# Two branches of softmax attention: projection moves on GpSimd's queue, and denominators moved and inverted ahead of the sums

## The chip, the core and the metric

One NeuronCore of a Trainium2 chip runs the whole program. The time is the device time of one execution, in microseconds (us). For the kernel before, three runs took 2023.84, 2019.86 and 2020.14 us; their median is 2020.14 us.

## The reference, cut to what matters

The same input x (2048 tokens, width 512) goes through two attention layers of 32 heads of width 16, and a gate mixes their outputs token by token. Branch a has one key and value head for all its query heads; branch b has its own for each.

```python
# B, S, D, H = 1, 2048, 512, 32; Dh = 16
g = sigmoid((x * gate_w).sum(-1, keepdims=True))
# a: k = x @ wk, v = x @ wv are shared by all 32 heads;  b: q, k, v per head from x @ wqkv
scores = einsum("bhqd,bhkd->bhqk", q, k) * Dh ** -0.5
p = softmax(scores, axis=-1)
o = einsum("bhqk,bhkd->bhqd", p, v)          # heads side by side, 512 wide
a_or_b = o.transpose(0, 2, 1, 3).reshape(B, S, D) @ wo
out = g * a + (1 - g) * b
```

The exponentials are the bulk: 2 branches x 32 heads x 2048 x 2048 of them.

## The kernel before, in words

**The stream of exps.** The work is cut into eight groups of eight heads, a0, b0, a1, b1 and so on to a3, b3. A group has two halves of 1024 queries. Within a half, four "banks" follow each other; a bank is four (head, block of 512 queries) pairs over all 16 tiles of 128 keys. ScalarE (ACT) takes two pairs' scores for one key tile at a time: one instruction on 128 x 1024 scores, called an exp below (line 533). There are 2048 of them, 256 to a group, 128 to a half, 32 to a bank. TensorE (PE) makes the scores of an exp (line 529) into one of two PSUM buffers, and multiplies the probabilities with the values (line 548, "P V") a few exps later. Ones stand beside the values, so the P V bank collects for each head 16 rows of sums and 16 rows of denominators. There is no pass for a maximum.

**The other work of PE** is put between the exps, one or two products of 216 planned ns at a time: projections of x to Q, K and V of the next head groups, twelve products each per block of 512 tokens (line 351; the helper's line 189 appears in the profile), and output projections, three products each (line 442, again line 189). They accumulate in that pair of the two P V bank pairs which is not in use ("spare"), so VectorE (DVE) has to empty a bank before PE can begin the next of them.

**After a projection** DVE adds the two half sums into a tile y (lines 193 and 194), clips it, and splits it into a high and a low fp16 part, hi and lo (lines 201 and 202). Then rows of hi and lo have to go to other partitions: for each Q or K tile of a head pair p, eight DMAs of 32 KB (line 338, function `lay`, "moves" below). A projection of 1024 tokens gives four `lay` calls. They go into a list, from which one is taken each three exps (line 124). All these DMAs are issued by SyncE's queue (SP), except the first ones of the program.

**After a P V bank** DVE copies it to a tile `raw` (lines 193, 194; `emptied`, line 553), and eight DMAs on SP move its 16-row pieces into oT (sums) and dT (denominators), alternating. When two banks are in, for each of four 128-token columns DVE runs `over`, the reciprocal of dT (line 462), and then `parts`: the product with oT, and the split into fp16 halves (lines 469 to 471). Then PE can make the output projection of these tokens (`o_unit`), and DVE adds it to the result (line 450).

**What sets the order.** All queues are in order. A planner (`_Tasks`) writes the program exp by exp: `now` counts exps, a clock adds planned ns for each piece, EXP is the planned length of an exp (904), `units` holds products with the earliest exp and a due exp, `side` holds DVE and GpSimd pieces with their earliest exp, and `moves` the `lay` calls. None of it waits for time on the chip; it sets the order alone.

**GpSimd (POOL)** splits each newly loaded weight into fp16 halves (`split_weight`, lines 205 to 207), about 12 exps into a half. Two or three buffers serve each kind of weight, so such a split can wait for PE to be done with an older weight.

Of the kernel before, what the change touches and what calls it, by code (L numbers as in the profile page):

```python
# [22 lines left out]
DH = 16  # L23
# [3 lines left out]
BLK = 512  # L27
ACT = 2
ROWS, COLS = 64, 32
EXP = 904  # L30
SCORES, HALF, PRODUCT = 213, 428, 216
FULL = 1500
LATE = 250
# [31 lines left out]
class _Tasks:  # L65
# [53 lines left out]
    def beside(self, until):  # L119
        while self.side and self.side[0][0] <= self.now and self.busy <= until:  # L120
            _, f, ns = self.side.popleft()
            f()
            self.given(ns)
        if self.moves and self.moved <= self.now - 3:
            self.moved = self.now
            self.moves.popleft()()

    def flush(self):
# [3 lines left out]
        while self.open or self.units or self.side:  # L132
# [5 lines left out]
            self.now += 100  # L138
            self.clock += 100 * EXP
            while self.product(1 << 20) and self.open:  # L140
# [12 lines left out]
def _fast(ctx, tc, x, wq_a, wk_a, wv_a, wo_a, wqkv_b, wo_b, gate_w, out, flag):  # L153
    nc = tc.nc
# [60 lines left out]
    todo = _Tasks()  # L215
# [158 lines left out]
    def q_units(src, gi, half, queues, late=None):  # L374
        def put(p):
            Q[src, gi, half, p] = ops.tile([P, 2 * BLK], F16, tag="Q", name=f"Q{src}{gi}{half}{p}", bufs=8)
            return Q[src, gi, half, p]

        return project(weights[src, gi, "q"], ("q", src, gi), f"{src}{gi}", f"q_{src}", 4 * gi + 2 * half, half,
                       ("hi", "lo", "hi", "lo"), put, queues, late)  # L380

    def k_units(gi, half, queues):
        def put(p):
            if half == 0:
                K[gi, p] = ops.tile([P, S], F16, tag="K", name=f"K{gi}{p}", bufs=4)
            return K[gi, p][:, half * 2 * BLK : (half + 1) * 2 * BLK]

        return project(weights["b", gi, "k"], ("k", "b", gi), f"k{gi}", "k_b", 4 * gi + 2 * half, half,
                       ("hi", "hi", "lo", "lo"), put, queues)

    def v_units(gi):

        w = weights["b", gi, "v"]

        def product(b, n):
            assert ("v", "b", gi) in ready
            c, (x_part, w_part) = n // 3, PARTS[n % 3]
            by_tiles(spare(), w[:, w_part, c * P : (c + 1) * P], xT[:, x_part, c, b * BLK : (b + 1) * BLK],
                     n == 0, n == 3 * NK - 1)
            if n < 3 * NK - 1:  # L400
                return
            y = ops.tile([P, BLK], F32, tag="y", name=f"yv{gi}{b}")
            v16 = ops.tile([P, 2, BLK], F16, tag="v16", name=f"v16{gi}{b}")
            added(y, spare(), UP ** -2)
            split(v16[:, 0], v16[:, 1], y)
            absmax("v_b", 4 * gi + b, y)
            todo.add([[lambda t=t: turned(b, v16, t) for t in range(4)]], todo.now + 4, todo.now, -400)

        def turned(b, v16, t):
            banks = spare()  # L410
            at = slice(t * DH * 4, (t + 1) * DH * 4)
            for part in range(2):
                for n in range(0, P, COLS):
                    for i, bank in enumerate(banks):
                        r = slice(ROWS * i, ROWS * (i + 1))
                        nc.tensor.matmul(bank[n : n + COLS, at], v16[r, part, t * P + n : t * P + n + COLS],
                                         ident16[r, r], start=t == part == 0, stop=t == 3 and part == 1)
            if t < 3:
                return
            for i, bank in enumerate(banks):  # L420
                o = bank[:, : 4 * ROWS].rearrange("p (t a b d) -> p t a b d", t=4, a=2, b=2)
                for hh in range(2):
                    nc.vector.tensor_scalar(vB[:, 4 * b : 4 * b + 4, 2 * i : 2 * i + 2, 2 * hh, :], o[:, :, :, hh, :],
                                            1 / UP, None, op0=ALU.mult)
            turns[gi] = turns.get(gi, 0) + 1
            if turns[gi] == 4:
                ready.add(("v", gi))

        return [[lambda b=b, n=n: product(b, n) for n in range(3 * NK)] for b in range(4)]

    turns = {}
    oT, dT, o16s = {}, {}, {}
# [23 lines left out]
    def norm_pieces(src, gi, half, t8, last):  # L456
        j, cols = t8 // 4, slice(t8 % 4 * P, (t8 % 4 + 1) * P)
        ends = last and half and j

        def over():  # L460
            d = dT[src, gi, half, j][:, cols]
            nc.vector.reciprocal(d, d)  # L462

        def parts():
            o, d = oT[src, gi, half, j][:, cols], dT[src, gi, half, j][:, cols]
            if t8 == 0:
                o16s[src, gi, half] = ops.tile([P, 2, 2 * BLK], F16, tag="o16", name=f"o16{src}{gi}{half}", bufs=3)
            o16 = o16s[src, gi, half][:, :, t8 * P : (t8 + 1) * P]
            nc.vector.scalar_tensor_tensor(o, o, UP, d, op0=ALU.mult, op1=ALU.mult)
            (nc.scalar.copy if ends else nc.vector.tensor_copy)(o16[:, 0], o)  # L470
            (nc.gpsimd if ends else nc.vector).tensor_sub(o16[:, 1], o, o16[:, 0])
            todo.add([o_unit(src, gi, 8 * half + t8, o16, last)], todo.now + 4,
                     todo.now + (64 if last and half else 300))

        return [over, parts]
# [30 lines left out]
    def gates():  # L506
# [9 lines left out]
    blocks = [(n, half, s, c, p, j, hh) for n in range(len(groups)) for half in range(2)  # L516
              for s, bank in enumerate(banks) for c in range(NT) for p, j, hh in bank]
# [35 lines left out]
    def emptied(m):  # L553
        quad = blocks[4 * m : 4 * m + 4]
        n, half, s, c = quad[0][:4]
        src, gi = groups[n]
        raw = ops.tile([P, BLK], F32, tag="raw", name=f"raw{src}{gi}{half}{s}", bufs=1)
        added(raw, aux[turn[0]], 1.0)
        j = quad[0][5]
        if s % 2 == 0:  # L560
            oT[src, gi, half, j] = ops.tile([P, BLK], F32, tag="oT", name=f"oT{src}{gi}{half}{j}")
            dT[src, gi, half, j] = ops.tile([P, BLK], F32, tag="dT", name=f"dT{src}{gi}{half}{j}")
        for i, (_, _, _, _, p, _, hh) in enumerate(quad):
            rows = slice((2 * p + hh) * DH, (2 * p + hh + 1) * DH)
            parts = (oT, dT) if src == "a" or hh == 0 else (dT, oT)
            for part, at in zip(parts, (32 * i, 32 * i + DH)):
                ends = 4 * m + 4 == len(blocks)
                queues = (nc.sync, nc.scalar, nc.sync, nc.scalar, nc.gpsimd) if ends else (nc.sync,)
                queues[at // DH % len(queues)].dma_start(part[src, gi, half, j][rows], raw[at : at + DH, :])  # L569
        last = n == len(groups) - 1  # L570
        if s % 2:
            todo.add_side([f for t8 in range(4 * j, 4 * j + 4) for f in norm_pieces(src, gi, half, t8, last)],
                          todo.now + (5 if last and half else 10), [950, 800])

    def flag_stats():
        absmax("v_a", 0, vA[:, :, :DH], AX.XY)
# [28 lines left out]
    def begin(n, half):  # L605

        src, gi = groups[n]
        now = todo.now
        start = lambda n, half: (512 * n + 256 * half) // ACT
        sync = (nc.sync,)  # L610
        if half == 0:
            todo.add(q_units(src, gi, 1, sync), now if n else 24, start(n, 1) - 24, 2200)
        if n == 0 and half == 0:
            todo.add_side(load_w(*groups[1]), now + 12, [0])
        if n + 2 < len(groups) and half:
            todo.add_side(load_w(*groups[n + 2]), now + 12, [0])
        if n + 1 == len(groups):
            if half:
                todo.add_side([flag_stats], now + 60, [9000])
                todo.add_side([flag_reduce], now + 75, [400])  # L620
                todo.add_side([flag_check], now + 90, [1500])
            return
        nxt = groups[n + 1]
        due = start(n + 1, 0) - 36
        if half == 0:
            if nxt[0] == "b":
                todo.add(k_units(nxt[1], 0, sync) + k_units(nxt[1], 1, sync), now + (12 if n else 40), due - 90, 2200)
                todo.add(v_units(nxt[1]), now + (12 if n else 40), due - 30, 1700)
        else:
            todo.add(q_units(*nxt, 0, sync), now + 6, due, 2200)  # L630

# [25 lines left out]
    while done < halves:  # L659
        u += 1  # L660
        todo.now, todo.clock = u, u * EXP
        if u < exps:
# [4 lines left out]
        for f in early.get(u, ()):  # L667
            f()
        end = (u + 1) * EXP
        if half_values(u) and done < u - 2 and u % 2:  # L670
# [147 lines left out]
```

## Time and profile before

| | before |
|---|---|
| median of three runs | 2020.14 us |
| the profiled execution's own time | 2015.9 us |
| its span, first to last instruction | 2014.1 us |
| busy: PE, ACT, DVE, POOL | 1872.3, 1897.1, 768.9, 92.6 us |
| mean granted TensorE clock | 0.98 |
| DMA issued by SP, mean busy share of the 16 engines | 11.6% |

The views used are: the page (busy time; groups of instructions with their count, mean and the idle time before them), the list of waits (who waited for whom: us in total, times, longest), and timelines of one engine (start, length, instruction; in brackets the idle time of the engine just before it and what ended it). "SPq" is the time in which SP's queue issues a DMA. In a timeline "x3" means that like instructions were merged in one row.

### The profile page before, as it was taken

The numbers are of one execution on the slowest core, as the hardware profiler recorded it, in microseconds if no ns is written. First come the engines' busy times: TensorE is split into PE (matmuls) and PEld (weight loads), VectorE is DVE, ScalarE is ACT, GpSimd is POOL, SyncE is SP. The second block draws the span as 40 slices with busy tenths as digits, with TensorE's granted clock in tenths as the row PEclk, the third lists the DMA queues.
The fourth block names the chain that finished last, engine by engine and source line by source line (L and its number), as shares of the span: only waits on it lengthen the run. The fifth ranks groups of instructions, "written<-read, shape, count | busy, mean of one in ns | idle before, by whom it ended". The sixth has DMA issues, their size and how long they took to land.

```text
span 2014.1 us, 127353 instructions
## 1 busy us (share of the span) xinstructions
PE 1872.3 (93%) x59664; PEld 1062.3 (53%) x59664; DVE 768.9 (38%) x1429; ACT 1897.1 (94%) x2071; POOL 92.6 (5%) x103
## 2 busy tenths in 40 slices
PE   7988998999998999999998999999999899999995
PEld 4544654554554655555454665555545465555442
DVE  4332443424143444434333344452423333444432
ACT  4987998999998999999998999999999899999994
POOL 5001000020000000020000000002000000000000
PEclk9999999999998999999999999999999899999997
DMA  4012011111011101111002201011101110111111
GB/s 139 12 39 54 15 25 29 27 29 35 14 33 41 36 21 26 35 31 28 21 16 47 47 11 36 18 28 35 35 12 29 40 29 16 34 29 36 35 32 32
DMA packets 55735, 65.00 MB, mean 32 GB/s; under 512 B 21440, under 2 KB 29632, under 8 KB 55200
## 3 DMA queue, kind: packets, MB, share of 16 engines
q1 hardware_dynamic: 53984, 55.66, 11.6%
q8 instruction: 469, 7.68, 1.6%
q0 software_dynamic: 528, 0.69, 0.2%
q14 instruction: 66, 0.54, 0.1%
q10 hardware_dynamic: 688, 0.43, 0.1%
HBM read 10.55 MB, written 4.19 MB: 7 GB/s over the span
## 4 chain that ended last, share of the span: by engine, by line
ACT 69%; PE 11%; issue 7%; SPq 7%; DVE 3%; DMA 2%; ACTq 0%; DVEq 0%; POOL 0%
ACT pr L533 69%; SPq L338 5%; PE aux L548 5%; PE sc L529 3%; PE aux L189 3%; SPq L569 2%; DMA dTa<-rawa 1%; DMA acc<-in_A_x_dram 0%; DVE acc L450 0%; DVE dTa L462 0%; DMA Qa<-hia 0%; DVE yk L194 0%; DVE xT L269 0%; PE aux L297 0%; DVE yk L193 0%
## 5 line engine op out<-in xcount | busy, mean ns | idle before, releaser
L533 ACT ACTIVATE pr<-sc 128x1024 f32<-128x1024 f32 x2048 | 1886.5, 1188 | 67.3 <-PE sc L529 66.3
L548 PE MATMUL aux<-pr,vA 64*32 64x256 f32 x16384 | 688.0, 379 | 3.9 <-issue 3.6
L548 PE MATMUL aux<-pr,vB 64*32 64x256 f32 x16384 | 648.9, 376 | 0.3 <-issue 0.2
L529 PE MATMUL sc<-Qa,kA 64*32 64x512 f16 x8192 | 457.3, 387 | 19.9
L529 PE MATMUL sc<-Qb,K 64*32 64x512 f16 x8192 | 427.0, 385 | 41.7
L529 PEld LDWEIGHTS <-K 64*32 64x32 f16 x8192 | 209.7, 89 | 385.5 <-issue 307.6
L548 PEld LDWEIGHTS aux<-pr,vA 64*32 64x32 f32 x16384 | 334.6, 106 | 60.6 <-issue 19.5
L529 PEld LDWEIGHTS <-kA 64*32 64x32 f16 x8192 | 209.1, 90 | 282.6 <-issue 211.1
L548 PEld LDWEIGHTS aux<-pr,vB 64*32 64x32 f32 x16384 | 310.6, 105 | 36.6 <-issue 1.8
L450 DVE SCALAR_TENSOR_TENSOR acc<-aux,gate_up,acc 128x512 f32<-128x512 f32 x240 | 180.1, 750 | 265.7 <-PE aux L189 251.7
L462 DVE RECIPROCAL dTa<-dTa 128x128 f32<-128x128 f32 x64 | 60.6, 946 | 170.5 <-DMA dTa<-rawa 170.5
L189 PE MATMUL aux<-xT,w16kb 64*32 64x512 f16 x1536 | 91.8, 393 | 28.9 <-DVE yk L193 27.7
L193 DVE TENSOR_SCALAR rawb<-aux 128x512 f32<-128x512 f32 x32 | 22.1, 689 | 217.3 <-PE aux L548 216.8
L189 PE MATMUL aux<-xT,w16vb 64*32 64x512 f16 x1536 | 89.5, 380 | 8.2 <-DVE yv L193 7.6
L189 PE MATMUL aux<-w16ob,o16b 64*32 64x512 f16 x1536 | 80.9, 391 | 13.3 <-ACT o16b L470 9.3
L462 DVE RECIPROCAL dTb<-dTb 128x128 f32<-128x128 f32 x64 | 60.5, 946 | 82.4 <-DMA dTb<-rawb 82.4
L189 PE MATMUL aux<-xT,w16qb 64*32 64x512 f16 x1536 | 82.1, 379 | 5.0 <-DVE yb L193 4.8
L189 PE MATMUL aux<-w16oa,o16a 64*32 64x512 f16 x1536 | 79.4, 376 | 0.0
L189 PE MATMUL aux<-xT,w16qa 64*32 64x512 f16 x1536 | 76.5, 380 | 0.0
L189 PEld LDWEIGHTS <-w16kb 64*32 64x32 f16 x1536 | 29.6, 96 | 48.2 <-issue 35.3
L193 DVE TENSOR_SCALAR yv<-aux 128x512 f32<-128x512 f32 x16 | 11.0, 688 | 113.0 <-PE aux L189 113.0
L193 DVE TENSOR_SCALAR yk<-aux 128x512 f32<-128x512 f32 x16 | 11.0, 690 | 102.2 <-PE aux L189 102.2
(130 smaller groups left out, 764.8 us busy)
## 6 DMA issues: line engine op xcount, KB each, us to landing
acc<-in_A_x_dram SPq DMA_DIRECT2D x16, 256.0 KB, 7.1
oTa<-rawa SPq DMA_DIRECT2D x128, 32.0 KB, 2.5
dTa<-rawa SPq DMA_DIRECT2D x128, 32.0 KB, 2.4
K<-hik SPq DMA_DIRECT2D x128, 32.0 KB, 2.0
K<-lok SPq DMA_DIRECT2D x128, 32.0 KB, 2.6
Qb<-hib SPq DMA_DIRECT2D x128, 32.0 KB, 2.6
Qb<-lob SPq DMA_DIRECT2D x128, 32.0 KB, 2.6
out_dram<-acc SPq DMA_DIRECT2D x16, 256.0 KB, 2.0
```

The lines of the kernel that those rows point to most:

```text
L189: nc.tensor.matmul(out[n : n + COLS], lhsT[r, n : n + COLS], rhs[r], start=start, stop=stop)
L193: nc.vector.tensor_scalar(dst, outs[0], scale, None, op0=ALU.mult)
L338: queues[(8 * p + n) % len(queues)].dma_start(op[to : to + DH].rearrange("d (a q) -> d a q", a=2), state[part][rows])
L450: nc.vector.scalar_tensor_tensor(acc[:, t], bank, g, acc[:, t], op0=ALU.mult, op1=ALU.add)
L462: nc.vector.reciprocal(d, d)
L529: nc.tensor.matmul(sc[a : a + COLS, i], k[r, c * P + a : c * P + a + COLS], Q[src, gi, half, p][r, j * BLK : (j + 1) * BLK], start=True, s ...
L533: nc.scalar.activation(probs[u][:, :m], sc[:, :m], AF.Exp, scale=SCALE / (UP * UP))
L548: nc.tensor.matmul(o[32 * i : 32 * i + 32, cols], v[r], probs[at // ACT][r, at % ACT, cols], start=c == half == 0, stop=c == NT - 1 and ha ...
L569: queues[at // DH % len(queues)].dma_start(part[src, gi, half, j][rows], raw[at : at + DH, :])
```

## The change

The DMAs of `lay` are issued by GpSimd's queue in place of SP's, and the planner takes a `lay` from the list each six exps. A bank's four denominator pieces are moved ahead of its four sum pieces. The reciprocals of four columns are planned at 10 exps after the bank and the rest (`parts`) at 13, each as a list of its own, in place of reciprocal and rest by turns from 10. In the last half both are planned at 4 in place of 5, and the last bank's eight moves go round SP, ACT and POOL. EXP is 916 in place of 904. The first Q projection of the program's second half may start at exp 21 (24 before), and the K and V projections of b0 at 24 (40 before).

```diff
-EXP = 904
+EXP = 916
...
-        if self.moves and self.moved <= self.now - 3:
+        if self.moves and self.moved <= self.now - 6:
...
-        for i, (_, _, _, _, p, _, hh) in enumerate(quad):
-            rows = slice((2 * p + hh) * DH, (2 * p + hh + 1) * DH)
-            parts = (oT, dT) if src == "a" or hh == 0 else (dT, oT)
-            for part, at in zip(parts, (32 * i, 32 * i + DH)):
-                ends = 4 * m + 4 == len(blocks)
-                queues = (nc.sync, nc.scalar, nc.sync, nc.scalar, nc.gpsimd) if ends else (nc.sync,)
-                queues[at // DH % len(queues)].dma_start(part[src, gi, half, j][rows], raw[at : at + DH, :])
+        ends = 4 * m + 4 == len(blocks)
+        queues = (nc.sync, nc.scalar, nc.gpsimd) if ends else (nc.sync,)
+        for a, part in enumerate((dT, oT)):
+            for i, (_, _, _, _, p, _, hh) in enumerate(quad):
+                rows = slice((2 * p + hh) * DH, (2 * p + hh + 1) * DH)
+
+                at = 32 * i + (DH if (src == "a" or hh == 0) == (part is dT) else 0)
+                queues[(4 * a + i) % len(queues)].dma_start(part[src, gi, half, j][rows], raw[at : at + DH, :])
         last = n == len(groups) - 1
         if s % 2:
-            todo.add_side([f for t8 in range(4 * j, 4 * j + 4) for f in norm_pieces(src, gi, half, t8, last)],
-                          todo.now + (5 if last and half else 10), [950, 800])
+            over, parts = zip(*[norm_pieces(src, gi, half, t8, last) for t8 in range(4 * j, 4 * j + 4)])
+            todo.add_side(over, todo.now + (4 if last and half else 10), [950])
+            todo.add_side(parts, todo.now + (4 if last and half else 13), [800])
...
-        sync = (nc.sync,)
+        pool = (nc.gpsimd,)
         if half == 0:
-            todo.add(q_units(src, gi, 1, sync), now if n else 24, start(n, 1) - 24, 2200)
+            todo.add(q_units(src, gi, 1, pool), now if n else 21, start(n, 1) - 24, 2200)
...
-                todo.add(k_units(nxt[1], 0, sync) + k_units(nxt[1], 1, sync), now + (12 if n else 40), due - 90, 2200)
-                todo.add(v_units(nxt[1]), now + (12 if n else 40), due - 30, 1700)
+                todo.add(k_units(nxt[1], 0, pool) + k_units(nxt[1], 1, pool), now + (12 if n else 24), due - 90, 2200)
+                todo.add(v_units(nxt[1]), now + (12 if n else 24), due - 30, 1700)
         else:
-            todo.add(q_units(*nxt, 0, sync), now + 6, due, 2200)
+            todo.add(q_units(*nxt, 0, pool), now + 6, due, 2200)
```

**What moves, first place: DVE, some 67 exps into the program.** The second P V bank of a0 is copied to raw, and near it the first K projection of b0 ends (tiles yk, hik, lok). Before:

```order
L193 TENSOR_SCALAR rawa_2272<-aux_82 128x512
L194 SCALAR_TENSOR_TENSOR rawa_2272<-aux_83,rawa_2272 128x512
L462 RECIPROCAL dTa_1429<-dTa_1429 128x128
L469 SCALAR_TENSOR_TENSOR oTa_1428<-oTa_1428,dTa_1429 128x128
L470 CAST o16a_2612<-oTa_1428 128x128
L471 TENSOR_TENSOR o16a_2612<-oTa_1428,o16a_2612 128x128
L193 TENSOR_SCALAR yk_2670<-aux_82 128x512
```

and now:

```order
L193 TENSOR_SCALAR yk_2341<-aux_84 128x512
L194 SCALAR_TENSOR_TENSOR yk_2341<-aux_85,yk_2341 128x512
L356 TENSOR_SCALAR yk_2341<-yk_2341 128x512
L201 TENSOR_SCALAR hik_2016<-yk_2341 128x512
L202 SCALAR_TENSOR_TENSOR lok_2017<-yk_2341,hik_2016 128x512
L198 TENSOR_REDUCE stats<-yk_2341 128x1
L193 TENSOR_SCALAR rawa_2386<-aux_82 128x512
L194 SCALAR_TENSOR_TENSOR rawa_2386<-aux_83,rawa_2386 128x512
L462 RECIPROCAL dTa_1534<-dTa_1534 128x128 x3
L193 TENSOR_SCALAR yk_2809<-aux_82 128x512
```

The reciprocal still stands ahead of a projection's copy out of its bank (yk). Three reciprocals now follow each other, and the products with oT come later.

**Second place: SP's queue, same bank.** Before, moves of Q stand ahead of the bank's pieces:

```order
L338 DMA Qa_2244<-hia_1495 16x1024
L338 DMA Qa_2244<-loa_1496 16x1024
L569 DMA oTa_1428<-rawa_2272 16x512
L569 DMA dTa_1429<-rawa_2272 16x512
L569 DMA oTa_1428<-rawa_2272 16x512
```

and now (from the four weights of b0 on):

```order
L225 DMA wob_538<-in_B_wo_dram 128x512
L570 DMA dTa_1534<-rawa_1530 16x512 x4
L570 DMA oTa_1533<-rawa_1530 16x512 x4
L570 DMA dTa_1534<-rawa_2386 16x512 x4
L570 DMA oTa_1533<-rawa_2386 16x512 x4
L570 DMA dTa_3270<-rawa_3266 16x512 x4
```

Nothing but pieces of P V banks, weights and, at the end, results is left on SP; the denominators' four go first.

**Third place: POOL's queue, in the second half of a1.** The split of a2's weights (w16qa, w16oa) stood between other splits before; now moves of b1's first Q half stand right behind it:

```order
L206 CAST w16qa_17216<-wqa_17214 128x512
L207 TENSOR_TENSOR w16qa_17216<-wqa_17214,w16qa_17216 128x512
L205 TENSOR_SCALAR woa_17217<-woa_17217 128x512
L206 CAST w16oa_17219<-woa_17217 128x512
L207 TENSOR_TENSOR w16oa_17219<-woa_17217,w16oa_17219 128x512
L338 DMA Qb_19464<-hib_18624 16x1024
L338 DMA Qb_19464<-lob_18625 16x1024
```

The rows of the splits are the same as before; what is new is that 32 moves wait behind them.

## The prediction

> **What bounds the kernel now.** I read the page first: who is busy, and what ends the waits.
>
> ```profile
> span 2014.1 us, 127353 instructions
> PE 1872.3 (93%) x59664; PEld 1062.3 (53%) x59664; DVE 768.9 (38%) x1429; ACT 1897.1 (94%) x2071; POOL 92.6 (5%) x103
> L533 ACT ACTIVATE pr<-sc 128x1024 f32<-128x1024 f32 x2048 | 1886.5, 1188 | 67.3 <-PE sc L529 66.3
> ```
>
> ACT's 2048 exps take 1886.5 us (0.921 us each, since they overlap); 127.6 us of the span are not exps. 67.3 us of that are idle time of ACT in front of an exp, nearly all of it ended by a score of PE. The rest is the start before the first exp, the tail behind the last, and small ACT work. The change adds and removes no exp, so only these 127.6 us can move. Next, the rows of ACT's timeline that have an idle time in front of them (in brackets) of several us, with those beside them that the sums below use: where do the 67.3 us lie?
>
> ```profile
> 52.61 13.05 ACT L533 ACTIVATE pr<-sc 128x1024 f32<-128x1024 f32 x14 [0.54 <-PE sc L529]
> 122.08 1.02 ACT L533 ACTIVATE pr<-sc 128x1024 f32<-128x1024 f32 x1 [7.74 <-PE sc L529]
> 123.78 1.02 ACT L533 ACTIVATE pr<-sc 128x1024 f32<-128x1024 f32 x1 [0.69 <-PE sc L529]
> 125.48 43.19 ACT L533 ACTIVATE pr<-sc 128x1024 f32<-128x1024 f32 x47 [0.67 <-PE sc L529]
> 191.06 1.02 ACT L533 ACTIVATE pr<-sc 128x1024 f32<-128x1024 f32 x1 [8.67 <-PE sc L529]
> 320.89 1.02 ACT L533 ACTIVATE pr<-sc 128x1024 f32<-128x1024 f32 x1 [5.81 <-PE sc L529]
> 323.88 291.60 ACT L533 ACTIVATE pr<-sc 128x1024 f32<-128x1024 f32 x318 [0.26 <-PE sc L529]
> 623.30 1.02 ACT L533 ACTIVATE pr<-sc 128x1024 f32<-128x1024 f32 x1 [7.82 <-PE sc L529]
> 1104.67 1.02 ACT L533 ACTIVATE pr<-sc 128x1024 f32<-128x1024 f32 x1 [8.35 <-PE sc L529]
> 1588.32 1.02 ACT L533 ACTIVATE pr<-sc 128x1024 f32<-128x1024 f32 x1 [7.98 <-PE sc L529]
> ```
>
> Six stalls hold 7.74 + 8.67 + 5.81 + 7.82 + 8.35 + 7.98 = 46.4 us. Short gaps follow each until PE is ahead again: 0.69 + 0.67 = 1.36 us at the first. With 1.36 at each, the six places cost 46.4 + 8.2 = 54.5 us. That leaves 66.3 - 54.5 = 11.8 us in small gaps, among them the first exps. In between, 318 exps ran in 291.6 us (0.917 each) in one row, beside PE's ordinary mix of work.
>
> What holds PE there? Its waits, in us, times and longest; then SP, DVE and PE at the first place:
>
> ```profile
> PE aux L189 <- DVE yk L193: 27.7, 4, 7.3
> PE aux L189 <- DVE yv L193: 7.6, 1, 7.6
> PE aux L189 <- DVE yb L193: 4.8, 1, 4.8
> ```
>
> ```profile
> 96.87 0.51 SPq L338 DMA_DIRECT2D Qa<-hia  x1
> ...
> 109.49 0.59 SPq L338 DMA_DIRECT2D Qa<-loa  x1
> 110.17 0.53 SPq L569 DMA_DIRECT2D oTa<-rawa  x1
> ...
> 115.56 0.58 SPq L569 DMA_DIRECT2D dTa<-rawa  x1
> ```
>
> ```profile
> 98.86 0.69 DVE L194 SCALAR_TENSOR_TENSOR rawa<-aux,rawa 128x512 f32<-128x512 f32 x1
> 117.58 0.95 DVE L462 RECIPROCAL dTa<-dTa 128x128 f32<-128x128 f32 x1 [18.02 <-DMA dTa<-rawa]
> ...
> 119.36 0.68 DVE L193 TENSOR_SCALAR yk<-aux 128x512 f32<-128x512 f32 x1
> ```
>
> ```profile
> 112.77 0.63 PE L548 MATMUL aux<-pr,vA 64*32 64x256 f32 x16
> 120.10 0.58 PE L189 MATMUL aux<-xT,w16kb 64*32 64x512 f16 x1 [6.71 <-DVE yk L193]
> ```
>
> Read backwards: PE, done at 113.4, waits 6.7 us for DVE to empty a bank (yk). DVE, in order, stands at a reciprocal until 117.58. That waits for the last denominator's DMA, issued at 115.56, though raw was ready at 99.55. SP was busy from 96.87 to 110.08 with sixteen moves of Q, 13.2 us in a row, and then sent the bank's eight pieces by turns. PE has six such waits, 27.7 + 7.6 + 4.8 us: one for each stall of ACT. So 54.5 us hang on one cause: moves ahead of denominators on SP.
>
> **The change part by part.** *Moves to POOL, denominators first.* SP then holds the bank's pieces with nothing in front. Eight of them took 110.17 to 116.14, 0.75 us each, on a queue that also had moves in flight. What a DMA takes from issue to landing (last number of the first two rows), and what POOL needed for moves at the program's start, with a copy of DVE amid them:
>
> ```profile
> dTa<-rawa SPq DMA_DIRECT2D x128, 32.0 KB, 2.4
> Qa<-loa POOLq DMA_DIRECT2D x4, 32.0 KB, 2.6
> 25.44 0.48 POOL L338 DMA_DIRECT2D Qa<-hia  x1
> 28.30 0.48 POOL L338 DMA_DIRECT2D Qa<-hia  x1
> 25.16 0.17 DVE L309 COPY kn<-kn 128x64 f16<-128x64 f16 x1
> ```
>
> Four denominators are in 4 x 0.75 + 2.4 = 5.4 us after raw, against 18.0 at the first place. The reciprocal is planned 10 exps (9.2 us) after the bank. Where a projection is copied out ahead of raw, as now at this place, raw comes later by yk's six instructions, at 0.68 each 4.1 us at most: 4.1 + 1.4 for raw itself + 5.4 = 10.9 us. DVE then stands still for under 2 us, and what is next behind, the copy of the second K block, is due only when PE ends it, 82 exps into the program against 67 for the bank (13.8 us). So all six stalls go: -54.5 us. If half of each stayed, -27; more than 54.5 cannot come from here.
>
> *What POOL pays.* In the profile it issued ten such moves, 0.48 us apart (25.44 to 28.30 is seven), two of them waiting for the eighth DMA before. A `lay` takes 3.9 us there against 6.0 on SP. POOL is busy 92.6 us; 736 moves (32 for each half of Q but the first, 64 for each K) at 0.48 add 353 us, to some 23%. The planner's six exps instead of three move nothing by themselves: a queue runs on as soon as its data is there. The tightest place is b0's first Q half: planned 17 exps (15.6 us) before its first scores, it needs about 3 us of DVE, sixteen moves for the first two tiles (7.7) and 2.6 for the landing, 13.3 in all. The cover is 2 us, so I cost it at nothing; without it, each 0.1 us a move costs 1.6 us, once.
>
> POOL's own waits come ahead of moves now:
>
> ```profile
> 754.37 0.61 POOL L206 CAST w16oa<-woa 128x512 f16<-128x512 f32 x1 [77.09 <-PE aux L189]
> ```
>
> This cast waits until PE has read b0's last output weights. The first Q half of b1 stands behind it. In PE's order that reading stands 33 exps (30 us) ahead of b1's first scores. The cast and the subtraction behind it take some 1.8 us, sixteen moves 7.7, the landing 2.6: 12.1. The cover is 18 us; cost 0, and a stall only from 1.6 us a move. The same holds at b2.
>
> *The start.* The second Q half of a0 may begin at exp 21, and its first products then stand ahead of exp 22's scores. They write a bank that DVE still reads:
>
> ```profile
> 55.98 0.64 PE L548 MATMUL aux<-pr,vA 64*32 64x256 f32 x16
> 57.34 0.41 DVE L319 COPY kA<-aux 128x512 f16<-128x512 f16 x1
> ```
>
> PE would be there at about 56.4 and waits until 57.75. With 0.2 for the product and 0.4 for the scores, exp 22 can start at 58.4. It was due at 57.2 (the row at 52.61 begins with exp 17, five of 0.917 earlier): +1.2, bounds 0 and 1.4.
>
> *Reciprocals four in a row, in the tail.* Behind the last exp nothing hides anything.
>
> ```profile
> 1992.14 0.95 DVE L462 RECIPROCAL dTb<-dTb 128x128 f32<-128x128 f32 x1 [3.79 <-DMA dTb<-rawb]
> 1988.65 0.71 POOL L569 DMA_DIRECT2D oTb<-rawb  x1 [38.86 <-DVE rawb L194]
> 1996.18 0.42 POOL L471 TENSOR_TENSOR o16b<-oTb,o16b 128x128 f16<-128x128 f32 x1 [6.82 <-issue]
> ```
>
> The last denominator is the second issue on its queue, not the third: 0.6 us earlier. Four reciprocals (3.8) instead of one come ahead of the first product, which moves from 1993.1 to about 1995.4. But the first output unit waits for POOL's low half at 1996.2 anyway, behind 6.8 us of POOL alone, and that moves by the 0.7 us of POOL's second DMA. +0.7 in all, bounds -1 and +3.
>
> *EXP and the other due times* shift where products stand. PE's count of products is the same, so I take the 11.8 us of small gaps as they are, plus 1 for less room (bounds -6 and +10).
>
> Sum: 2014.1 - 54.5 + 1.2 + 0.7 + 1 = 1962.5 us of span. The profiled execution's own time was 2015.9, and the median of the runs lies 4.2 above that, 6.0 above the span. Taken over: 1968.5.
>
> [...]
>
> **The rivals.** *Stalls stay in part* (14%). Denominators might still come late, or the reciprocals of a batch might hold a projection's copy. Against it: 5.4 us against 9.2. For it: DVE is in order, and its 38% comes in bursts. At a third of the 54.5: 1968.5 + 18 = 1986.5. PE taking over as bound in dense stretches (it is 93% busy) ends between the two.
>
> *POOL becomes the slow queue: slower than before* (4%). In an a group, POOL issues 32 moves of Q, 64 of K and 16 of b's first Q tiles before b begins: 112 in the some 226 exps (207 us) after the first projection's copy, or 1.85 us each. From there on every 0.1 us costs 11 us in each of four a groups. At 2.1 us a move that is 4 x 112 x 0.25 = 112 us, against the 52 won: 2080. From about 1.97 it is slower. For it: POOL is the engine with the least on record, ten moves. Against it: 0.48, a quarter of that.
>
> *It does nothing* (4%): the stalls reach DVE by another way, such as the weights' DMAs on SP, and come back at the same length: 2020. Against it: the six waits of PE and SP's thirteen us of moves.
>
> **How the numbers follow.** My forecast has 78%, with a range of its own of 1958 to 1975. The range for 8 in 10 is 1957 (nearly all of the small gaps gone too) to 1986 (a third of the stalls left). About 0.2%, 4 us, is what a measurement of this kernel can tell from no change. Faster 0.92 (the forecast and the first rival), same 0.04, slower 0.04.
>
> **What would show it.** In the changed profile: ACT's idle time before exps falls to some 14 us, with no gap over 3 us past the first 60; PE's waits on yk, yv and yb vanish; POOL's moves stand at about 0.48 us; SP is idle much of the time; the denominators' issues are four in a row right behind raw. I am wrong if POOL's moves stand over a microsecond apart, if a gap of several us stands at exp 256, 768, 1280 or 1792 (late Q or K), or if DVE still waits for dT with PE behind it.

## The result, and the profile after

The changed kernel takes 1962.65 us (median of four runs, 1959.14 to 1963.78) against 2021.99 for the kernel before (four runs): a ratio of 0.970, with a 95% interval of 0.968 to 0.972. The forecast was 1968.5 us, with 1957 to 1986 around it. The profiled execution took 1959.1 us, its span is 1956.9. The page, then four rows of ACT's timeline after the start, among them the longest idle time there:

```profile
span 1956.9 us, 127404 instructions
PE 1857.9 (95%) x59664; PEld 1060.7 (54%) x59664; DVE 756.9 (39%) x1429; ACT 1895.2 (97%) x2071; POOL 444.7 (23%) x840
L533 ACT ACTIVATE pr<-sc 128x1024 f32<-128x1024 f32 x2048 | 1884.6, 1191 | 12.6 <-PE sc L529 11.7
```

```profile
52.50 13.05 ACT L533 ACTIVATE pr<-sc 128x1024 f32<-128x1024 f32 x14 [0.54 <-PE sc L529]
65.41 98.49 ACT L533 ACTIVATE pr<-sc 128x1024 f32<-128x1024 f32 x107
...
228.31 406.40 ACT L533 ACTIVATE pr<-sc 128x1024 f32<-128x1024 f32 x442 [0.50 <-PE sc L529]
...
1084.17 10.51 ACT L533 ACTIVATE pr<-sc 128x1024 f32<-128x1024 f32 x11 [0.79 <-PE sc L529]
```

ACT's idle time before exps fell from 67.3 to 12.6 us. The six stalls are gone, and no gap past the first 50 us is as long as 0.8. PE's waits on yk, yv and yb at line 193 no longer stand in its list of waits. At the first place, the timeline of SP and DVE now reads:

```profile
100.58 0.69 DVE L194 SCALAR_TENSOR_TENSOR rawa<-aux,rawa 128x512 f32<-128x512 f32 x1
...
101.30 3.39 SPq L570 DMA_DIRECT2D dTa<-rawa  x4
104.73 3.30 SPq L570 DMA_DIRECT2D oTa<-rawa  x4
107.61 2.58 DVE L462 RECIPROCAL dTa<-dTa 128x128 f32<-128x128 f32 x3 [6.34 <-DMA dTa<-rawa]
...
112.83 0.69 DVE L193 TENSOR_SCALAR yk<-aux 128x512 f32<-128x512 f32 x1 [2.64 <-PE aux L189]
```

The reciprocal still waits, 6.34 us where it was 18.02. But behind it DVE now waits for PE at yk (the last bracket), where PE waited for DVE before. Where the moves went, by the groups of instructions:

```profile
L338 POOL DMA_DIRECT2D Qb<-hib x128 | 62.3, 486 | 359.5 <-DVE hib L201 181.7 <-PE sc L529 173.0 <-issue 3.0
L338 POOL DMA_DIRECT2D K<-hik x128 | 61.5, 485 | 109.3 <-DVE hik L201 102.4 <-DMA K<-hik 4.0 <-issue 2.8
```

486 ns each: the price that ten moves showed before holds for the mean of all. The idle time in front of POOL's moves is long, and means that their queue ran dry: it waited for DVE's halves, or for PE to be done with an old Q tile.

One execution of those told of below was slow, one of six of the kernel with the moves alone, VectorE's subtraction and banks by turns: it took 5866.68 us at a granted clock of 0.275, where the other five had 0.992 to 0.994, and no run shows why.

### The profile page after: what moved, and what is told of

Same layout as the page of the kernel before. It is cut to its first block, busy times and chain, and to the rows that moved or that the text cites. A ratio compares the mean times of both kernels' runs of the same rounds, so it can differ in the third digit from the quotient of the medians.

```text
span 1956.9 us, 127404 instructions
## 1 busy us (share of the span) xinstructions
PE 1857.9 (95%) x59664; PEld 1060.7 (54%) x59664; DVE 756.9 (39%) x1429; ACT 1895.2 (97%) x2071; POOL 444.7 (23%) x840
## 4 chain that ended last, share of the span: by engine, by line
ACT 83%; issue 8%; PE 7%; DVE 2%; DMA 0%; SPq 0%; POOL 0%; ACTq 0%; DVEq 0%
ACT pr L533 82%; PE aux L548 3%; PE sc L529 2%; PE aux L189 2%; DVE xT L269 0%; DVE acc L450 0%; DMA acc<-in_A_x_dram 0%; PE aux L416 0%; ACT xT L268 0%; DVE dTb L462 0%; PE pt L264 0%; PE aux L297 0%; DMA dTb<-rawb 0%; PE aux L318 0%; PE aux L264 0%
## 5 line engine op out<-in xcount | busy, mean ns | idle before, releaser
L533 ACT ACTIVATE pr<-sc 128x1024 f32<-128x1024 f32 x2048 | 1884.6, 1191 | 12.6 <-PE sc L529 11.7
L338 POOL DMA_DIRECT2D Qa<-hia x118 | 57.8, 489 | 449.4 <-PE sc L529 299.1
L338 POOL DMA_DIRECT2D Qb<-hib x128 | 62.3, 486 | 359.5 <-DVE hib L201 181.7
L189 PE MATMUL aux<-w16ob,o16b 64*32 64x512 f16 x1536 | 80.3, 391 | 15.1 <-ACT o16b L470 13.2
L189 PE MATMUL aux<-xT,w16vb 64*32 64x512 f16 x1536 | 93.8, 376 | 0.1
L338 POOL DMA_DIRECT2D K<-hik x128 | 61.5, 485 | 109.3 <-DVE hik L201 102.4
L189 PE MATMUL aux<-xT,w16kb 64*32 64x512 f16 x1536 | 82.2, 376 | 0.0
L462 DVE RECIPROCAL dTa<-dTa 128x128 f32<-128x128 f32 x64 | 55.6, 918 | 59.8 <-DMA dTa<-rawa 59.8
L462 DVE RECIPROCAL dTb<-dTb 128x128 f32<-128x128 f32 x64 | 55.4, 916 | 52.9 <-DMA dTb<-rawb 52.9
```

The source lines that it names most:

```text
L189: nc.tensor.matmul(out[n : n + COLS], lhsT[r, n : n + COLS], rhs[r], start=start, stop=stop)
L338: queues[(8 * p + n) % len(queues)].dma_start(op[to : to + DH].rearrange("d (a q) -> d a q", a=2), state[part][rows])
L533: nc.scalar.activation(probs[u][:, :m], sc[:, :m], AF.Exp, scale=SCALE / (UP * UP))
```

## The experiments

The theory, from the prediction, is called *queue* below: the stalls are moves that stand ahead of denominators on SP. The rivals: *order* (denominators first, and reciprocals in a list of their own, carry the gain) and *GpSimd alone* (any move on SP holds the pieces up). The expectations name a replay: SP's queue worked through from the rows of before, 0.83 us a move, 2.4 us to land, 0.95 us a reciprocal, with the planner's exps for the rest. All results:

| kernel | ACT idle before exps | median us | ratio to before | 95% |
|---|---|---|---|---|
| changed | 12.6 | 1962.65 | 0.970 | 0.968 to 0.972 |
| moves on GpSimd alone | 11.9 | 1955.53 | 0.969 | 0.966 to 0.971 |
| changed, moves on SP | 16.5 | 1962.75 | 0.973 | 0.970 to 0.975 |
| six exps alone | 40.8 | 1986.43 | 0.983 | 0.980 to 0.986 |
| denominators first alone | 56.6 | 2008.14 | 0.996 | 0.994 to 0.997 |
| planner's edits alone | 65.4 | 2011.22 | 0.998 | 0.996 to 0.999 |
| two DMAs a move | 26.5 | 1975.99 | 0.981 | 0.978 to 0.985 |
| four DMAs a move | 306.2 | 2260.39 | 1.123 | 1.119 to 1.126 |
| two tail edits | 10.2 | 1958.81 | 0.973 | 0.970 to 0.975 |
| changed, again | 9.5 | 1955.87 | 0.971 | 0.970 to 0.973 |
| moves on GpSimd alone, again | 10.6 | 1955.17 | 0.970 | 0.969 to 0.971 |
| moves on GpSimd, denominators first, VectorE's subtraction, banks by turns | 9.9 | 1957.31 | 0.971 | 0.970 to 0.973 |
| changed, with three tail edits | 9.3 | 1956.78 | 0.971 | 0.970 to 0.973 |

The rows after the first stand in groups of four, each on one chip. Before took 2014 to 2022 us in the medians of the groups, so across groups only ratios compare. The idle time is that of one profiled execution.

**Moves on GpSimd, and nothing else.**

```diff
-        sync = (nc.sync,)
+        sync = (nc.gpsimd,)
```

> Before with one edit: the moves of Q and K on GpSimd's queue, all else old (three exps between moves, pieces by turns, reciprocal and norm in one list, EXP 904). Theory 'queue' (moves ahead of denominators on SP make the stalls): SP holds the bank's pieces alone, the last denominator lands some 8 x 0.75 + 2.4 = 8.4 us after raw, against a reciprocal planned 9.2 us behind it. All six stalls go: ACT idle before exps 12 to 18 us, profiled execution 1960 to 1968, 0.972 to 0.976 of before. Rival 'order' (the gain needs the denominators first and the four reciprocals apart from the sums): at least half of the 54.5 us stays, ACT idle 38 or more, 1986 or more. Rival 'POOL full' (moves three exps apart are too dense for GpSimd at 0.48 us): a gap of several us at exps 256, 768, 1280 and 1792.

Idle 11.9 us, 1958.28 for the profiled execution, ratio 0.969: one word brings the whole gain, and *order* falls. The pieces still go by turns; in the timeline raw is done at 100.51, the last piece's issue begins at 105.37, and the reciprocal runs 8.0 us after raw (8.4 expected):

```profile
99.82 0.69 DVE L194 SCALAR_TENSOR_TENSOR rawa<-aux,rawa 128x512 f32<-128x512 f32 x1
...
105.37 0.92 SPq L569 DMA_DIRECT2D dTa<-rawa  x1
108.49 0.95 DVE L462 RECIPROCAL dTa<-dTa 128x128 f32<-128x128 f32 x1 [7.97 <-DMA dTa<-rawa]
...
111.91 0.69 DVE L193 TENSOR_SCALAR yk<-aux 128x512 f32<-128x512 f32 x1 [1.55 <-PE aux L189]
```

**The changed kernel with its moves back on SP.**

```diff
-        pool = (nc.gpsimd,)
+        pool = (nc.sync,)
```

> After with one edit undone: the moves back on SP, everything else new (six exps between moves, denominators first, new due times). Theory 'queue', replayed with the rows of before (0.83 us a move on SP, 2.4 to land, 0.95 a reciprocal): eight moves take SP 6.6 us and come at most each 5.5 us (six exps), so at most one or two groups of moves stand ahead of a bank's four denominators; the replay leaves 2.3 us in two places (exps 151 and 272). ACT idle 12 to 20, profiled execution 1958 to 1967. So the queue theory says that the move to GpSimd isn't needed for the gain once the rest is done. Rival 'GpSimd alone' (it is the other engine that does it, any move on SP holds the pieces up): at least half of the stalls stays, idle 38 or more, 1985 or more.

Idle 16.5 us, 1961.44: as *queue* had it, and *GpSimd alone* falls too. SP and DVE at the first place:

```profile
102.89 0.58 SPq L338 DMA_DIRECT2D Qa<-loa  x1
103.58 2.96 SPq L570 DMA_DIRECT2D dTa<-rawa  x4
...
108.01 2.58 DVE L462 RECIPROCAL dTa<-dTa 128x128 f32<-128x128 f32 x3 [6.92 <-DMA dTa<-rawa]
```

The moves end at 103.5, 2.4 us after raw is done (101.09, the reciprocal's start less its wait). Past the start ACT's timeline has two gaps of over 1 us:

```profile
172.74 3.77 ACT L533 ACTIVATE pr<-sc 128x1024 f32<-128x1024 f32 x4 [1.33 <-PE sc L529]
...
279.81 1.02 ACT L533 ACTIVATE pr<-sc 128x1024 f32<-128x1024 f32 x1 [2.73 <-PE sc L529]
```

They look like the two places of the replay, but they are not. The second stands at b0's first scores, at exp 257 and not 272, and PE waits there for a late move of Q, not for DVE:

```profile
PE sc L529 <- DMA Qb<-lob: 2.5, 1, 2.5
```

At the first, PE goes on at 171.59 after a pause of 1.12 us for which the profile shows no event, while DVE waits for its denominators until 172.48. So the 2.3 us that the replay left to late denominators did not come, and that two gaps stand near its places is chance. What the spacing costs on SP is Q, which comes 2.5 us late once.

So there are two ways to keep the denominators from waiting: another queue, or fewer moves at a time together with the rest of the change. The second is a little worse: on the same chip its median lies 7.2 us above that of the moves alone. In the two profiled executions, which lie 3.2 us apart, the idle time differs by 4.6 us, of which the two gaps are 4.1; the rest of the 7.2 is open.

**Six exps between moves, and nothing else, on SP.**

```diff
-        if self.moves and self.moved <= self.now - 3:
+        if self.moves and self.moved <= self.now - 6:
```

> Before with one edit: six exps instead of three between groups of eight moves, still on SP, pieces by turns, old due times. Theory 'queue', by the same replay (which gives before's six stalls at their places, 5 to 17 us each): fewer moves stand ahead, the stall at the first place goes, those at exps 143 and 272 stay at 5 to 7 us and the other three shrink to 2.4. 19 us left of 54.5: ACT idle 27 to 40, profiled execution 1975 to 1988. Rival 'order' and rival 'GpSimd alone': spacing changes nothing, idle 60 to 70, 2009 to 2018.

Idle 40.8, 1990.76 for the profiled execution and 1986.43 in the median: half of the gain, and 0.8 and 2.8 us outside what *queue* gave. Stalls of 4.20, 5.12, 4.33 and 4.16 us are left, and two are gone (the first and the last).

**Denominators first, and nothing else.** The loop over the pieces is that of the changed kernel (dT, then oT); moves stay on SP.

> Before with one edit: the bank's four denominators ahead of its four sums, moves on SP as before. Theory 'queue', by the same replay: each stall ends 4 x 0.8 = 3.3 us earlier, no more, since the sixteen moves stay ahead: 31 us left of 54.5, ACT idle 38 to 50, profiled execution 1988 to 1999. Rival 'order' (denominators first carry the gain): idle under 25, under 1975.

Idle 56.6 us: a miss for both theories' numbers. I had 31 us left of the stalls' 54.5, and all but 10.7 of them stayed. Five of the six stalls shrank, by 1.0 to 2.9 us. The one at 616 us stayed (7.67 long, 7.82 before), on DVE:

```profile
610.61 0.95 DVE L462 RECIPROCAL dTa<-dTa 128x128 f32<-128x128 f32 x1 [16.48 <-DMA dTa<-rawa]
613.08 0.29 DVE L469 SCALAR_TENSOR_TENSOR oTa<-oTa,dTa 128x128 f32<-128x128 f32 x1 [1.52 <-DMA oTa<-rawa]
...
613.88 0.68 DVE L193 TENSOR_SCALAR yk<-aux 128x512 f32<-128x512 f32 x1
```

The reciprocal waits less, but the product with the sums stands right behind it in this order, and waits another 1.52 us for the sums, which now go last. From raw (594.13, the reciprocal's start less its wait) to yk it is 19.75 us. In the kernel before it was 19.9 at the same place:

```profile
600.01 0.69 DVE L194 SCALAR_TENSOR_TENSOR rawa<-aux,rawa 128x512 f32<-128x512 f32 x1
...
620.59 0.68 DVE L193 TENSOR_SCALAR yk<-aux 128x512 f32<-128x512 f32 x1
```

My replay had let only denominators hold DVE. That the separate lists would take this second wait away is argued: no run has denominators first with these lists and all else old.

**The planner's edits alone**: EXP, the due times, and reciprocals and sums in lists of their own; queue, spacing and pieces as before.

> Before with the planner's edits alone: EXP 916, the earlier due times (21 and 24), reciprocals and sums in lists of their own; moves on SP three exps apart, pieces by turns. Theory 'queue', by the replay: as many moves stand ahead as before, at partly other places (82, 151, 272, 592, 1104, 1616): 59 us against 54 in the replay of before. ACT idle 55 to 75, profiled execution 2003 to 2022. Rival 'order': idle under 40, under 1988.

Idle 65.4, 2014.0, and 0.998 in the ratio: next to nothing, as *queue* had it. The stalls stand at 127.39 (8.88), 200.48 (8.41), 322.04 (4.02), 623.20 (6.92), 1104.91 (8.52) and 1587.05 (8.67), close to where they were.

**What GpSimd's price may be.** The prediction gave a threshold: no loss below some 1.6 us a move but for b0's first Q half, and a full queue from 1.85. Each move is sent as two, then as four DMAs (the edit for two, shortened):

```diff
-                    queues[...].dma_start(op[to : to + DH].rearrange("d (a q) -> d a q", a=2), state[part][rows])
+                    for e in range(2):
+                        queues[...].dma_start(op[to : to + DH, e * BLK : (e + 1) * BLK], state[part][rows, e])
```

> After with each move sent as two DMAs of half the length on GpSimd. If a DMA costs GpSimd 0.48 us whatever its size, a move costs 0.96: POOL is busy 445 + 353 = 800 us, and by the prediction's sum (cover 2 us at b0's first Q half, sixteen moves ahead of it) one stall of 16 x 0.48 - 2 = 5.7 us stands at exp 256, none at 768, 1280 and 1792; profiled execution 1963 to 1967. If the price goes by size, nothing changes: POOL 445 us, 1957 to 1962.

> After with each move sent as four DMAs of a quarter on GpSimd: some 1.92 us a move if each costs 0.48. Past the prediction's 1.85 us a move (112 moves in 207 us): every a group falls behind by 112 x 0.07 = 8 us at its end, b0's first Q half by 16 x 1.44 - 2 = 21 us, and those behind the w16oa cast at b1 and b2 by 16 x 1.44 - 18 = 5. Stalls at exps 256, 768, 1280 and 1792 of together 30 to 70 us, profiled execution 1990 to 2030. If the cover was more than I took, 1960 to 1975; if the price goes by size, 1957 to 1962.

The groups of POOL, at two DMAs and at four:

```profile
L339 POOL DMA_DIRECT2D Qb<-hib x256 | 123.3, 486 | 256.9 <-DVE hib L201 171.3 <-PE sc L530 79.7 <-issue 5.2
```

```profile
L339 POOL DMA_DIRECT2D Qb<-hib x512 | 246.1, 488 | 72.3 <-PE sc L531 39.1 <-DVE hib L201 25.5 <-issue 7.3
```

486 to 488 ns in the mean, for 32, 16 and 8 KB alike: the price is per DMA, 0.97 us a move with two and 1.95 with four. With two, b0's first scores wait, on PE:

```profile
287.05 0.40 PE L530 MATMUL sc<-Qb,K 64*32 64x512 f16 x4 [0.65 <-DMA Qb<-lob]
...
289.37 0.40 PE L530 MATMUL sc<-Qb,K 64*32 64x512 f16 x4 [1.93 <-DMA Qb<-lob]
```

and ACT's gap there is 2.63 us, not 5.7 (the profiled execution took 1976.40 us, not 1963 to 1967); at exps 768, 1280 and 1792 there is none over 1.2. The cover was thus 7.7 - 2.6 = 5 us rather than 2. The rest of the loss lies at the start: gaps of 3.73 and 7.65 us, the second of which I had not foreseen. PE waits 7.01 us for kA there, and DVE ahead of kA waits for POOL:

```profile
60.75 0.69 DVE L198 TENSOR_REDUCE stats<-wqb 128x1 f32<-128x512 f32 x1 [2.80 <-POOL wqb L205]
...
64.24 0.69 DVE L198 TENSOR_REDUCE stats<-wob 128x1 f32<-128x512 f32 x1 [2.80 <-POOL wob L205]
...
64.84 0.41 DVE L319 COPY kA<-aux 128x512 f16<-128x512 f16 x1
...
65.31 0.62 PE L189 MATMUL aux<-xT,w16qa 64*32 64x512 f16 x7 [7.01 <-DVE kA L319]
```

With four it is this wait that breaks the kernel. DVE's, PE's and ACT's rows at the first large stall, ACT's at the next two,

```profile
314.27 0.69 DVE L198 TENSOR_REDUCE stats<-wqa 128x1 f32<-128x512 f32 x1 [61.79 <-POOL wqa L205]
...
319.10 0.58 PE L189 MATMUL aux<-xT,w16vb 64*32 64x512 f16 x1 [55.24 <-DVE yv L193]
...
321.07 1.02 ACT L535 ACTIVATE pr<-sc 128x1024 f32<-128x1024 f32 x1 [56.28 <-PE sc L531]
...
878.85 1.02 ACT L535 ACTIVATE pr<-sc 128x1024 f32<-128x1024 f32 x1 [49.80 <-PE sc L531]
...
1421.80 1.02 ACT L535 ACTIVATE pr<-sc 128x1024 f32<-128x1024 f32 x1 [50.83 <-PE sc L531]
```

and the wait in the list of waits (us in all, times, longest):

```profile
DVE stats L198 <- POOL wqa L205: 176.2, 3, 61.8
```

DVE takes the largest value of each new weight, after POOL has scaled it (line 205). On POOL that scaling stands behind the moves. DVE, in order, waits 61.8 us for it, and so does all that stands behind on DVE, PE and ACT. It does so three times, once in each of ACT's three long gaps, which hold 157 of its 306.2 us. What the expectation had summed is there too: the gaps at exps 256 and 257, 769, 1281 and 1793, where PE waits for b's Q, are together 30 us (30 to 70 expected). The wait for the weights was not in it. The kernel is slower than before by 0.123 of its time, some 250 us, where by my rival's arithmetic 1.95 us a move costs 4 x 112 x 0.1 = 45 us of the 52 won, so that it would still be a little faster than before.

**Is the rest worth anything?** The changed kernel and the moves alone once more, now on one chip.

> The changed kernel itself, on the chip of the three others of this group, since the earlier comparison of the two (1962.7 against 1955.5 for the moves alone) went over two chips. Theory 'rest is neutral' (denominators first, split lists, six exps and the new due times add nothing to the move to GpSimd): 1955 to 1960 here, equal to the moves alone within 3 us. Theory 'rest costs': 4 to 7 us above the moves alone.

> Before with the moves on GpSimd and nothing else, a second time, beside the changed kernel. 'Rest is neutral': within 3 us of the changed kernel. 'Rest costs': 4 to 7 us below it, as 1955.5 against 1962.7 had it.

1955.87 (1954.54 to 1958.90) against 1955.17 (1952.20 to 1956.58), five runs each: no difference that can be told. With the moves on GpSimd, the six exps, denominators first, the separate lists and the due times add nothing that these runs can tell. The 7 us between the two in the first runs did not come back on one chip; of them, 4.3 us lay between the medians of before itself in those two groups (2021.99 and 2017.7).

**The tail.** Behind the last exp nothing is hidden. The rows after it in the changed kernel:

```profile
1933.13 3.39 DVE L462 RECIPROCAL dTb<-dTb 128x128 f32<-128x128 f32 x4 [3.27 <-DMA dTb<-rawb]
...
1937.05 1.06 PE L189 MATMUL aux<-w16ob,o16b 64*32 64x512 f16 x16 [8.73 <-ACT o16b L470]
...
1938.34 0.42 POOL L471 TENSOR_TENSOR o16b<-oTb,o16b 128x128 f16<-128x128 f32 x1 [6.98 <-issue]
```

Two edits for the last bank's four tiles: VectorE subtracts in GpSimd's place, and each tile's sums follow its own reciprocal.

```diff
-            (nc.gpsimd if ends else nc.vector).tensor_sub(o16[:, 1], o, o16[:, 0])
+            nc.vector.tensor_sub(o16[:, 1], o, o16[:, 0])
...
+            if ends:
+                todo.add_side([f for two in pieces for f in two], todo.now + 4, [950, 800])
```

> After with two edits in the tail alone (the last bank's four tiles): VectorE instead of GpSimd subtracts for the low half, and each tile's sums follow its own reciprocal instead of all four reciprocals. From the rows of after: the first output unit waits 8.73 us of PE for four reciprocals (3.39) and its low half for GpSimd's 6.98 us that no event explains. Theory 'tail': first products 3 x 0.85 = 2.5 us earlier, the low half 3.5 to 4 earlier, and the four units no longer one behind another by 3.7 us each; the end of the span 3 to 5 us earlier: tail 25 to 27 us behind the last exp against 29.7, profiled execution 1954 to 1956.5. Rival: the copying out and the output's DMAs set the end, under 1 us. Everything before the last exp as in after.

A third edit: output products by turns in both pairs of banks. It is also put, with VectorE's subtraction, on the kernel with the moves alone (there with the denominators first as well; each tile's sums follow their own reciprocal in that kernel anyway).

```diff
+                turn[0] ^= todo.ending
                 state["ps"] = spare()
```

> The changed kernel with VectorE's subtraction, sums behind each reciprocal, and the banks by turns, all in the tail. The run with the first two of these ended 27.0 us behind the last exp against 29.7. With the banks by turns the last two tiles' products don't wait for VectorE (1.35 and 1.02 us there): tail 25 to 26 us, 3.5 to 5 us under the changed kernel beside it. Rival: under 2 us, since the output's DMAs set the end.

> Before with the moves on GpSimd, denominators first, VectorE's subtraction for the low halves of the last bank, and in the tail the output products of each tile in the other pair of banks than those of the tile ahead. Theory 'tail': first output products without GpSimd's 6.85 us, and PE no longer waits 0.9 us and more per tile for VectorE to read the bank: 3 to 6 us under the moves alone. Rival: the copying out on VectorE (four times 1.6 us) sets the end anyway, 1 to 3 us.

From the last exp to the end it is 27.0 us with two edits and 25.5 with three, against 29.7 in the changed kernel, as expected; on the moves alone it is 25.5 against 28.8. The times are misses all the same. With two edits the profiled execution took 1959.73 us (1954 to 1956.5 expected), and the other two medians are no lower than those of their kernels: 1956.78 and 1957.31 beside 1955.87 and 1955.17. What the tail won is lost at the start. POOL's and PE's timelines with three edits:

```profile
10.41 0.28 POOL masks.py:199 TENSOR_SCALAR_AFFINE_SELECT ident<-ident 128x128 f32<-128x128 f32 x1 [9.48 <-issue]
...
10.75 1.54 PE L264 MATMUL pt<-ident,acc 128*128 128x128 f32 x6 [10.75 <-DMA acc<-in_A_x_dram]
...
34.95 2.88 ACT L534 ACTIVATE pr<-sc 128x1024 f32<-128x1024 f32 x3
```

with, in the list of waits, the weight load (PEld) of these first products of PE:

```profile
PEld pt L264 <- POOL ident masks.py:199: 10.7, 1, 10.7
```

and those of the changed kernel beside it:

```profile
1.23 0.29 POOL masks.py:199 TENSOR_SCALAR_AFFINE_SELECT ident<-ident 128x128 f32<-128x128 f32 x1 [0.29 <-POOL ident masks.py:197]
...
4.05 1.09 PE L264 MATMUL pt<-ident,acc 128*128 128x128 f32 x4 [4.05 <-DMA acc<-in_A_x_dram]
...
28.23 2.88 ACT L533 ACTIVATE pr<-sc 128x1024 f32<-128x1024 f32 x3
```

POOL builds the identity 9.2 us later, PE begins 6.7 us later, and the first exp comes 6.7 us later. All three kernels without the subtractions on POOL show it (POOL's gap is 9.48 to 9.59 us), none of the others does (0.29). Against the same kernel without the tail's edits their first exp is 5.2 to 6.7 us late, which is more than the 2.7 to 4.3 us that the tail had won.

## Why the prediction was right, point by point

**The cause.** Right: six stalls from one cause, moves ahead of denominators on SP. One word that takes the moves off SP's queue removes all of them. With the moves left on SP, fewer at a time remove half, denominators first removes 10.7 us, and all the other edits together remove nearly all. A piece's time from issue to landing did not fall (dT of branch a: 2.4 us before, 2.6 after), so it was the issue that came late. The term of -54.5 us measured -54.7 for all of ACT's idle time before exps, the start and the small gaps included. For these the sum had +1.2 and +1 besides, which left 15.0 us of idle time against the 12.6 measured: 2.4 us too high.

**Denominators first.** Right in its place, with sizes off: four took 6.3 us (101.30 to the reciprocal), not 5.4, in the main since an issue took 0.85 us and not 0.75. In the changed kernel it was also without effect: the eight by turns are early enough once SP is free.

**What POOL pays.** Nothing, as predicted, at 486 ns and 23% busy: among 757 us of DVE's work the six groups of moves kept 485 to 489 ns in the mean, and no move took more than 602. A `lay` on SP took 6.6 us, by the 13.2 us of sixteen moves, and not 6.0, but no term used it. Three points of this step were off. The cover at b0's first Q half, by the gap with two DMAs a move, is 5 us, not 2. That six exps in place of three move nothing holds for POOL's queue; on SP they alone brought half of the gain, with which the prediction did not reckon. And the list of what waits behind POOL's moves was not complete: I named POOL's weight splits as something that delays moves, and not that moves delay the splits, for which DVE waits at line 198. At 0.48 us this costs nothing (DVE has no such wait in the changed kernel); at 0.97 it stalls the start, at 1.95 it costs far more than the rival's 45 us. So that rival lacked the larger part of the mechanism and had its price wrong: it put the break-even at 1.97 us a move, and at 1.95 the kernel is 12% slower than before.

**The start: +1.2, measured 0.** This step failed. The first products of the second Q half did come ahead of exp 22's scores, but kA was copied earlier. DVE's row of the kn copy before was slow, and in the changed kernel it was not:

```profile
53.47 1.16 POOL L207 TENSOR_TENSOR w16ob<-wob,w16ob 128x512 f16<-128x512 f32 x1
53.49 1.17 DVE L310 COPY kn<-kn 128x64 f16<-128x64 f16 x1
```

```profile
52.90 0.18 DVE L310 COPY kn<-kn 128x64 f16<-128x64 f16 x1
...
55.76 0.41 DVE L319 COPY kA<-aux 128x512 f16<-128x512 f16 x1
...
56.26 0.42 PE L189 MATMUL aux<-xT,w16qa 64*32 64x512 f16 x8
```

kA ended at 56.17, PE came at 56.26, and nothing waited. I had carried over a time from one execution, in which the copy ran beside POOL's instruction in the first row and ended with it.

**The tail: +0.7, measured +1.3** (28.4 us behind the last exp before, 29.7 after). Right in kind: POOL's first subtraction, 10.5 us behind the last exp before and 11.1 after, came 0.65 us later, as forecast, and the four reciprocals hide ahead of it. The other half of the 1.3 us comes behind it, where the sum had nothing.

**The sum.** 1962.5 us of span against 1956.9. The difference is 2.4 of idle time (above), 1.9 of exps that took 1884.6 instead of 1886.5, and a first exp at 28.42 instead of 30.60, less 0.6 of tail. I had moved neither of the middle two. The exps' 1.9 us fit the gaps that went: ACT stands idle for PE's scores 43 times before and 24 times after, and an exp behind a gap takes 1.02 us where exps in a row come 0.917 apart, which makes some 19 x 0.1 us. The first exp's 2.2 us may be chance: in the profiles of the other kernels with a move in one DMA and GpSimd's subtractions it came at 28.2 to 30.2 us. The runs' median lies 3.5 us above the profiled time; I had 4.2.

## What to carry to other kernels

When an in-order engine waits for a DMA, look at what was issued ahead of it on the same queue: a late issue, not a slow transfer, made 54 us here, and one transfer class on another idle queue ended it. Before work is put on a queue, list both what its own entries wait for and which engines wait for the work that now stands behind it; here the full queue hurt most by the second list (three waits of DVE with four DMAs a move, 176.2 us together). And judge an edit at the end of a program by the whole time: here three such edits won what they should at the end, and the start lost more.

## What the runs showed of the hardware that was not expected

- A DMA took GpSimd's queue 485 to 489 ns in the mean of each group, at 32 KB (the changed kernel), 16 KB (two DMAs a move) and 8 KB (four) alike, so splitting a move in two doubled its price, from 0.486 to 0.97 us. SP's issues of 32 KB in the kernel before took 0.51 us at best and 0.59 in the median, and in the changed kernel 0.85 in the mean of the four in a row shown above.
- After `partition_all_reduce`, GpSimd's next ordinary instruction (the first subtraction in the tail) started 6.8 to 7.4 us after the DMA issue ahead of it in ten profiles: 6.82 before, 6.98 in the changed kernel, 6.85 with the moves alone, 7.4 with six exps alone. Part of this is a wait for ACT's copy of the sums, but that ended 2.42 us ahead of the start before, 1.34 in the changed kernel and 2.47 with the moves alone, so in these it doesn't set it. In the three profiles of kernels without such an instruction, the first `affine_select` waits 9.48 to 9.59 us, in the others 0.29. No event explains the rest of the first gap or the second, and that the two have one cause was not shown.
- Copies of 128x64 on DVE (kn, lines 309 and 310), otherwise 0.17 or 0.18 us, took 1.17 in the profile before (line 310) and 1.14 with two DMAs a move (line 309). Both times GpSimd's last instruction of a split (`TENSOR_TENSOR`, line 207) had started less than 0.2 us ahead, and the copy ended within 0.04 us of its end. Beside other instructions of a split such a copy took up to 0.61 us (line 310 in the changed kernel, beside line 205). No run was made to test it.
